# A fused forward and backward kernel: the joint stage laid out with d on partitions, with `grad_out` transposed by DMA

## The chip, the cores and the metric

The kernel runs on one core of one Trainium2 chip. The metric is device time in microseconds (us), taken over several executions; the profiled span, from the first to the last instruction of one execution, is about 2 us shorter. Before the change three runs gave a median of 1255.49 us (1254.1 to 1255.69). Some executions of a kernel fall in a slower state; runs are called fast or slow accordingly, and only fast runs are compared here. A ratio is the mean time of one kernel's fast runs over the mean time of the other's fast runs of the same rounds, on the same chip. It is therefore not quite the ratio of the medians quoted beside it.

## The reference, cut to what matters

The kernel computes the output of a small transducer model and the gradients of all its inputs. Two strided convolutions with GELU turn `x` into `f` with 4000 rows of 256 per batch. Then comes the joint stage, and the backward pass of everything.

```python
B, T, D, K, U = 2, 16000, 256, 3, 8              # all tensors are bf16
def _fwd_reference(x, w1, w2, g, w_f, w_g, w_o):
    ...                                          # two convolutions with stride 2: f is [2, 4000, 256]
    fe = jnp.einsum("btd,de->bte", f, w_f)
    ge = jnp.einsum("bud,de->bue", g, w_g)
    j = jnp.tanh(fe[:, :, None, :] + ge[:, None, :, :])      # [2, 4000, 8, 256]
    return jnp.einsum("btud,dv->btuv", j, w_o)

def reference(x, w1, w2, g, w_f, w_g, w_o, grad_out):        # grad_out is [2, 4000, 8, 256]
    _out, _vjp = jax.vjp(_f, x, w1, w2, g, w_f, w_g, w_o)
    return (_out, *_vjp(grad_out))
```

For the joint stage this means five things per batch. The output is `j @ w_o`. The gradient of `j` is `grad_out @ w_o.T`. It is multiplied by `1 - j*j` (the kernel keeps the negative of this product and calls it NGZ). NGZ summed over `u` is the gradient of `fe`; NGZ summed over `t` is the gradient of `ge`. The gradient of `w_o` is `j.T @ grad_out`, summed over all rows.

## The kernel before

A chunk is 512 rows of `t` (`TBF`), a block is 128 rows; each batch has eight chunks. `JT` holds tanh with d on the 128 partitions and comes straight from ACT. Everything else was computed with t on partitions. So PE transposed both `JT` (to `JR`) and `grad_out` (`GO_R` to `GOT`), by matmuls with the identity into f32 PSUM tiles of 512 columns, which ACT and DVE copied out as bf16.

```python
    def pe_transpose4(ps_pool, dst_ap, srcs, eng=None):
        ps = ps_pool.tile([P, 4, P], FP32, name="tr4_ps")
        for j, src in enumerate(srcs):
            nc.tensor.matmul(ps[:, j, :], lhsT=src, rhs=ident[:], start=True, stop=True)     # L153
        ...
        if eng == "act":
            nc.scalar.copy(out=dst_ap, in_=ps[:])                                            # L158
        else:
            nc.vector.tensor_copy(out=dst_ap, in_=ps[:])                                     # L160
    ...
        ps_fe = ...tile_pool(name="ps_fe", bufs=1, ...)       # PSUM pools of the joint stage
        ps_oj = ...tile_pool(name="ps_oj", bufs=2, ...)       # shared by O_ps and GJ_ps
        ps_tr = ...tile_pool(name="ps_tr", bufs=2, ...)
        ...
        def emit_reductions(NGZ_tb, tbg):                     # sums over t, then over u
            for u in range(U):
                for dt in range(KT):
                    nc.tensor.matmul(NGGE_ps[:, dt, u:u + 1], lhsT=NGZ_tb[:, u, dt * P:(dt + 1) * P],
                                     rhs=ones[:, 0:1], start=..., stop=...)                  # L319
            for dt in range(KT):
                for u in range(U):
                    nc.tensor.matmul(NGFE_ps[:, dt, :], lhsT=NGZ_tb[:, u, dt * P:(dt + 1) * P],
                                     rhs=ident[:], start=(u == 0), stop=(u == U - 1))        # L325
            nc.scalar.copy(out=NGFE_T[:, :, tcol:tcol + P], in_=NGFE_ps[:])
        ...
            for tbl in range(ntb):                            # each block of 128 rows
                ...                                           # GO_R loaded by DMA
                for g_ in range(U // 2):
                    srcs = [JT[:, kt, tbl, 2 * g_ + j, :] for j in range(2) for kt in range(KT)]
                    pe_transpose4(ps_tr, JR[:, 2 * g_:2 * g_ + 2, :, :], srcs, eng=("act" if g_ % 2 == 0 else "dve"))
                nc.vector.tensor_tensor(out=JSQ[:], in0=JR[:], in1=JR[:], op=ALU.mult)
                for g_ in range(U // 2):
                    srcs = [GO_R[:, 2 * g_ + j, kt * P:(kt + 1) * P] for j in range(2) for kt in range(KT)]
                    pe_transpose4(ps_tr, GOT[:, 2 * g_:2 * g_ + 2, :, :], srcs, eng="dve")
                for up in range(U // 2):
                    O_ps = ps_oj.tile([P, 2, V], FP32, name="OJ_ps")
                    ...                  # 4 matmuls of 256 columns: JT x WO       L390
                    GJ_ps = ps_oj.tile([P, 2, D], FP32, name="OJ_ps")
                    ...                  # 4 matmuls of 256 columns: GOT x WOT     L396
                    ...                  # 4 matmuls of 256 columns: JR x GO_R, summed in GWO_ps   L402
                    nc.scalar.copy(out=OUT_SB[:, 2 * up:2 * up + 2, :], in_=O_ps[:])         # L405
                    nc.vector.scalar_tensor_tensor(out=NGZ[:, 2 * up:2 * up + 2, :],         # L406
                                                   in0=JSQ[...], scalar=1.0, in1=GJ_ps[:],
                                                   op0=ALU.subtract, op1=ALU.mult)
                    ...                  # reductions of the block before; tanh of the next chunk on ACT, L345
```

Of the kernel before, what the change touches and what calls it, by code (L numbers as in the profile page):

```python
# [21 lines left out]
def kernel(  # L22
# [19 lines left out]
    nc = tc.nc  # L42
# [95 lines left out]
    ACC_GWO = accp.tile([P, KT, V], FP32, name="ACC_GWO")  # L138
    NGGE_all = accp.tile([P, B, KT, U], FP32, name="NGGE_all")
    GR8 = accp.tile([U, B, D], BF16, name="GR8")  # L140
# [9 lines left out]
    def pe_transpose4(ps_pool, dst_ap, srcs, eng=None):  # L150
        ps = ps_pool.tile([P, 4, P], FP32, name="tr4_ps")
        for j, src in enumerate(srcs):
            nc.tensor.matmul(ps[:, j, :], lhsT=src, rhs=ident[:], start=True, stop=True)  # L153
        if eng is None:
            eng = "act" if tr_ctr[0] % 2 == 0 else "dve"
            tr_ctr[0] += 1
        if eng == "act":
            nc.scalar.copy(out=dst_ap, in_=ps[:])  # L158
        else:
            nc.vector.tensor_copy(out=dst_ap, in_=ps[:])  # L160

    def pe_transpose8(ps_pool, dst_ap, srcs, eng=None):
        ps = ps_pool.tile([P, 8, P], FP32, name="tr8_ps")
        for j, src in enumerate(srcs):
            nc.tensor.matmul(ps[:, j, :], lhsT=src, rhs=ident[:], start=True, stop=True)  # L165
        if eng is None:
            eng = "act" if tr_ctr[0] % 2 == 0 else "dve"
            tr_ctr[0] += 1
# [4 lines that stand above are left out]
# [20 lines left out]
    for b in range(B):  # L193
# [107 lines left out]
        jtp = cctx.enter_context(tc.tile_pool(name="jtp", bufs=2))  # L301
        jtb = cctx.enter_context(tc.tile_pool(name="jtb", bufs=3))
        jtb2 = cctx.enter_context(tc.tile_pool(name="jtb2", bufs=2))
        ps_fe = cctx.enter_context(tc.tile_pool(name="ps_fe", bufs=1, space=bass.MemoryType.PSUM))
        ps_oj = cctx.enter_context(tc.tile_pool(name="ps_oj", bufs=2, space=bass.MemoryType.PSUM))
        ps_tr = cctx.enter_context(tc.tile_pool(name="ps_tr", bufs=2, space=bass.MemoryType.PSUM))
        ps_red = cctx.enter_context(tc.tile_pool(name="ps_red", bufs=1, space=bass.MemoryType.PSUM))
        ps_gge = cctx.enter_context(tc.tile_pool(name="ps_gge", bufs=1, space=bass.MemoryType.PSUM))
        ps_gwo = cctx.enter_context(tc.tile_pool(name="ps_gwo", bufs=1, space=bass.MemoryType.PSUM))
        GWO_ps = ps_gwo.tile([P, KT, V], FP32, name="GWO_ps")  # L310
        NGGE_ps = ps_gge.tile([P, KT, U], FP32, name="NGGE_ps")
        acc_state = {"n": 0, "n_gge": 0}
        n_acc_total = n_tb_total * U * KT

        def emit_reductions(NGZ_tb, tbg):
            for u in range(U):
                for dt in range(KT):
                    n = acc_state["n_gge"]
                    nc.tensor.matmul(NGGE_ps[:, dt, u:u + 1], lhsT=NGZ_tb[:, u, dt * P:(dt + 1) * P],  # L319
                                     rhs=ones[:, 0:1], start=(n == 0), stop=(n == n_acc_total - 1))  # L320
                    acc_state["n_gge"] = n + 1
            NGFE_ps = ps_red.tile([P, KT, P], FP32, name="NGFE_ps")
            for dt in range(KT):
                for u in range(U):
                    nc.tensor.matmul(NGFE_ps[:, dt, :], lhsT=NGZ_tb[:, u, dt * P:(dt + 1) * P],  # L325
                                     rhs=ident[:], start=(u == 0), stop=(u == U - 1))
            tcol = tbg * P
            nc.scalar.copy(out=NGFE_T[:, :, tcol:tcol + P], in_=NGFE_ps[:])

        def emit_fe(jc):  # L330
            t0 = jc * TBF
            JT = jtp.tile([P, KT, NTB, U, P], BF16, name="JT")
            fes = []
            for mt in range(KT):
                FE_ps = ps_fe.tile([P, TBF], FP32, name="FE_ps")
                for kt in range(KT):
                    nc.tensor.matmul(FE_ps[:, :], lhsT=WF[:, kt, mt * P:(mt + 1) * P],
                                     rhs=FT[:, kt, t0:t0 + TBF], start=(kt == 0), stop=(kt == KT - 1))
                fes.append(FE_ps)
            return JT, fes  # L340

        def tanh_gen(JT, fes):
            for mt in range(KT):
                for u in range(U):
                    nc.scalar.activation(out=JT[:, mt, :, u, :],  # L345
                                         in_=fes[mt][:, :].rearrange("p (tb t) -> p tb t", t=P),
                                         func=ACT.Tanh, bias=GE[:, mt, u:u + 1], scale=1.0)
                    yield

        JT_cur, fes = emit_fe(0)  # L350
        for _ in tanh_gen(JT_cur, fes):
            pass
        pending = None
        for jc in range(n_jchunks):
            ntb = NTB
            JT = JT_cur
            if jc + 1 < n_jchunks:
                JT_next, fes_next = emit_fe(jc + 1)
                tgen = tanh_gen(JT_next, fes_next)
            else:  # L360
                JT_next, tgen = None, None
            n_tanh_per_tb = (KT * U + ntb - 1) // ntb
            for tbl in range(ntb):
                tbg = jc * NTB + tbl
                tg0 = tbg * P
                Mv = max(0, min(P, MQ - tg0))
                GO_R = jtb.tile([P, U, V], BF16, name="GO_R")
                if Mv < P:
                    nc.gpsimd.memset(GO_R[:], 0.0)
                if Mv > 0:  # L370
                    nc.gpsimd.dma_start(out=GO_R[:Mv].rearrange("p u v -> p (u v)"),  # L371
                                        in_=grad_out[b, tg0:tg0 + Mv].rearrange("t u v -> t (u v)"))
                JR = jtb.tile([P, U, KT, P], BF16, name="JR")
                for g_ in range(U // 2):
                    srcs = [JT[:, kt, tbl, 2 * g_ + j, :] for j in range(2) for kt in range(KT)]
                    pe_transpose4(ps_tr, JR[:, 2 * g_:2 * g_ + 2, :, :], srcs, eng=("act" if g_ % 2 == 0 else "dve"))
                JSQ = jtb2.tile([P, U, KT, P], BF16, name="JSQ")
                nc.vector.tensor_tensor(out=JSQ[:], in0=JR[:], in1=JR[:], op=ALU.mult)
                GOT = jtb.tile([P, U, KT, P], BF16, name="GOT")
                for g_ in range(U // 2):  # L380
                    srcs = [GO_R[:, 2 * g_ + j, kt * P:(kt + 1) * P] for j in range(2) for kt in range(KT)]
                    pe_transpose4(ps_tr, GOT[:, 2 * g_:2 * g_ + 2, :, :], srcs, eng="dve")
                OUT_SB = jtb.tile([P, U, V], BF16, name="OUT_SB")
                NGZ = jtb.tile([P, U, D], BF16, name="NGZ")
                for up in range(U // 2):
                    O_ps = ps_oj.tile([P, 2, V], FP32, name="OJ_ps")
                    for j in range(2):
                        u = 2 * up + j
                        for kt in range(KT):
                            nc.tensor.matmul(O_ps[:, j, :], lhsT=JT[:, kt, tbl, u, :], rhs=WO[:, kt, :],  # L390
                                             start=(kt == 0), stop=(kt == KT - 1))
                    GJ_ps = ps_oj.tile([P, 2, D], FP32, name="OJ_ps")
                    for j in range(2):
                        u = 2 * up + j
                        for kt in range(KT):
                            nc.tensor.matmul(GJ_ps[:, j, :], lhsT=GOT[:, u, kt, :], rhs=WOT[:, kt, :],  # L396
                                             start=(kt == 0), stop=(kt == KT - 1))
                    for j in range(2):
                        u = 2 * up + j
                        for dt in range(KT):  # L400
                            n = acc_state["n"]
                            nc.tensor.matmul(GWO_ps[:, dt, :], lhsT=JR[:, u, dt, :], rhs=GO_R[:, u, :],  # L402
                                             start=(n == 0), stop=(n == n_acc_total - 1))
                            acc_state["n"] = n + 1
# [18 lines left out]
            if tgen is not None:  # L423
                for _ in tgen:
                    pass
# [270 lines left out]
```

## Time and profile before

| Reading | Value |
|---|---|
| Median of the runs | 1255.49 us |
| Joint stages (138–447 and 744–1052 us) | 309 and 308 us, half the span |
| PE busy in the first of them | 297 of 309 us |
| DVE, ACT, DMA in it | 239 us, 190 us, 30% |
| Joint stage per 512 rows | 37.03 us |

The joint stage's pace is read from the starts of the `GWO_ps` matmuls of successive chunks in the steady part of the stage. All paces below are taken this way. Successive chunks of before alternate between 36.2 and 37.3 us, so its mean comes out anywhere between 36.6 and 37.1 us, depending on the block that one counts from; 37.03 lies at the upper end, and sums built on it are good to about 0.3 us.

The page's first two parts show the busy time of each engine over the whole span, and the span in 40 slices (tenths of busy time, and the granted clock of PE). Profile of before:

```profile
PE 1090.8 (87%) x11147; PEld 861.4 (69%) x11196; DVE 859.9 (69%) x1254; ACT 648.3 (52%) x1023; POOL 190.6 (15%) x346
...
PE   3865599999999988799987749999999998878995
...
DVE  2999488778888875333369977787878887734232
...
PEclk9998599999999999999999978999999999999998
DMA  9766233233242264146447323333333224622552
```

PE shows nines in the two joint stages (slices 6 to 14 and 25 to 33, counted from 1), the clock has its top digit there but for an 8 in slice 25, and DMA is at 2 to 4 tenths in the first of them. The view by stretches gives the same in numbers. Its columns are the stretch in us, its length, then busy time and instruction count of PE, PE's weight loads, DVE, ACT and POOL, then granted clock, DMA share and GB/s. Before, the two joint stages; the stage behind each is called D here:

```profile
138.00:447.00 309.00, 297.43 (x3607) 256.72 (x3623) 238.67 (x356) 189.80 (x353) 36.46 (x66) 0.97 0.30 108
744.00:1052.00 308.00, 295.74 (x3605) 256.24 (x3621) 242.15 (x360) 190.75 (x354) 37.31 (x68) 0.98 0.31 109
```

The groups of instructions give the durations that the prediction is built of: busy us, mean ns of one, and the idle time of the engine before them with what ended it. Before:

```profile
L405 ACT CAST OUT_SB<-OJ_ps 128x512 bf16<-128x512 f32 x256 | 152.4, 595 | 155.8 <-PE OJ_ps L390 149.1
L406 DVE SCALAR_TENSOR_TENSOR NGZ<-JSQ,OJ_ps 128x512 bf16<-128x512 bf16 x256 | 169.6, 682 | 83.2 <-PE OJ_ps L396 83.0
L345 ACT ACTIVATE JT<-FE_ps,GE 128x512 bf16<-128x512 f32 x256 | 163.7, 723 | 12.4 <-PE NGFE_ps L325 5.0
L160 DVE CAST GOT<-tr_ps 128x512 bf16<-128x512 f32 x256 | 165.5, 683 | 3.9 <-PE tr_ps L153 2.1
L402 PE MATMUL GWO_ps<-GO_R,JR 128*128 128x256 bf16 x1024 | 164.5, 275 | 0.3
L170 ACT CAST FNg<-tr_ps 128x1024 bf16<-128x1024 f32 x32 | 32.4, 1012 | 146.5 <-PE tr_ps L165 146.5
L172 DVE CAST GFR<-tr_ps 128x1024 bf16<-128x1024 f32 x32 | 39.2, 1224 | 68.9 <-PE tr_ps L165 68.9
```

DVE spends 165.5 us of the two stages on nothing but copying transposed `grad_out` out of PSUM. PE's mean of 275 ns is the length of one 256-column matmul's record, whose end is modelled; the starts are 109 ns apart, and the starts are what a sum of work must use.

### The profile page before, as it was taken

Reading aid. Unit: us, or ns where it says so; the run is one execution under the profiler, and the core shown is the slowest. Engines: PE = TensorE matmul, PEld = TensorE weight load, DVE = VectorE, ACT = ScalarE, POOL = GpSimd, SP = SyncE. Lnnn points to the kernel's source line nnn. Section 1 sums busy time; section 2 is a strip of 40 time slices with the busy share of each in tenths; the row PEclk is TensorE's granted clock in tenths of the full one; section 3 lists DMA queues with packets and bytes.
Section 4 is the critical chain, followed back from the end, with each engine's and each line's share of the span. In section 5 each row is a group of like instructions: output and inputs, shape, how many; then the busy total and the mean of one; then the engine's idle time right before and its main releaser. Section 6 shows DMA issues by size and latency. Waiting matters only on the chain.

```text
span 1253.1 us, 26205 instructions
## 1 busy us (share of the span) xinstructions
PE 1090.8 (87%) x11147; PEld 861.4 (69%) x11196; DVE 859.9 (69%) x1254; ACT 648.3 (52%) x1023; POOL 190.6 (15%) x346
## 2 busy tenths in 40 slices
PE   3865599999999988799987749999999998878995
PEld 1333388888888845688843327888888885567884
DVE  2999488778888875333369977787878887734232
ACT  2887656676555401222258877666556642022223
POOL 0122011111111101023211211111111110101331
PEclk9998599999999999999999978999999999999998
DMA  9766233233242264146447323333333224622552
GB/s 175 188 180 175 80 114 124 103 109 129 102 134 103 90 225 150 51 136 205 149 106 191 116 107 121 117 121 111 127 111 126 102 105 148 226 70 78 197 190 83
DMA packets 122517, 165.27 MB, mean 132 GB/s; under 512 B 74304, under 2 KB 91232, under 8 KB 122400
## 3 DMA queue, kind: packets, MB, share of 16 engines
q0 software_dynamic: 34304, 123.39, 28.1%
q1 hardware_dynamic: 88096, 40.20, 13.1%
q8 instruction: 87, 1.43, 0.5%
q14 instruction: 30, 0.25, 0.1%
HBM read 75.41 MB, written 71.31 MB: 117 GB/s over the span
## 4 chain that ended last, share of the span: by engine, by line
PE 67%; DVE 16%; ACT 9%; issue 6%; DMA 2%; SPq 1%; another core or an unknown queue 0%; DVEq 0%; POOL 0%; ACTq 0%; POOLq 0%
PE tr_ps L153 9%; PE OJ_ps L390 9%; PE OJ_ps L396 8%; PE GWO_ps L402 8%; PE psE_t L594 7%; PE NGFE_ps L325 5%; DVE g_inner L178 3%; PE tr_ps L165 3%; ACT JT L345 3%; ACT FNg L170 3%; PE psA_t L245 2%; DVE g_rr L189 2%; PE NGGE_ps L319 2%; DVE g_oms L190 2%; PE GWF_ps L546 2%
## 5 line engine op out<-in xcount | busy, mean ns | idle before, releaser
L405 ACT CAST OUT_SB<-OJ_ps 128x512 bf16<-128x512 f32 x256 | 152.4, 595 | 155.8 <-PE OJ_ps L390 149.1
L406 DVE SCALAR_TENSOR_TENSOR NGZ<-JSQ,OJ_ps 128x512 bf16<-128x512 bf16 x256 | 169.6, 682 | 83.2 <-PE OJ_ps L396 83.0
L345 ACT ACTIVATE JT<-FE_ps,GE 128x512 bf16<-128x512 f32 x256 | 163.7, 723 | 12.4 <-PE NGFE_ps L325 5.0
L160 DVE CAST GOT<-tr_ps 128x512 bf16<-128x512 f32 x256 | 165.5, 683 | 3.9 <-PE tr_ps L153 2.1
L402 PE MATMUL GWO_ps<-GO_R,JR 128*128 128x256 bf16 x1024 | 164.5, 275 | 0.3
L390 PE MATMUL OJ_ps<-WO,JT 128*128 128x256 bf16 x1024 | 160.6, 273 | 4.9 <-ACT JT L345 1.5
L396 PE MATMUL OJ_ps<-WOT,GOT 128*128 128x256 bf16 x1024 | 154.0, 272 | 0.7
L600 DVE CAST GX_SB<-psE_t 128x512 bf16<-128x512 f32 x64 | 44.2, 691 | 125.7 <-ACT GX_SB L598 76.0
L245 PE MATMUL psA_t<-XC,W_81 128*128 128x512 bf16 (+1 forms) x377 | 93.7, 400 | 37.2 <-DVE HTe L182 18.3
L160 DVE CAST JR<-tr_ps 128x512 bf16<-128x512 f32 x128 | 88.0, 687 | 42.4 <-PE tr_ps L153 40.7
L390 PEld LDWEIGHTS <-JT 128*128 128x128 bf16 x1024 | 96.3, 98 | 27.7 <-issue 10.5
L153 PE MATMUL tr_ps<-ident,JT 128*128 128x128 bf16 x1024 | 101.6, 221 | 10.1 <-ACT JT L345 4.3
L170 ACT CAST FNg<-tr_ps 128x1024 bf16<-128x1024 f32 x32 | 32.4, 1012 | 146.5 <-PE tr_ps L165 146.5
L598 ACT CAST GX_SB<-psE_t 128x512 bf16<-128x512 f32 x64 | 37.5, 587 | 130.2 <-PE psE_t L594 87.4
L396 PEld LDWEIGHTS <-GOT 128*128 128x128 bf16 x1024 | 93.7, 98 | 13.0 <-issue 0.6
L153 PE MATMUL tr_ps<-ident,GO_R 128*128 128x128 bf16 x1024 | 99.7, 220 | 0.6 <-ACT JR L158 0.2
L402 PEld LDWEIGHTS <-JR 128*128 128x128 bf16 x1024 | 93.7, 99 | 8.4
L153 PEld LDWEIGHTS <-JT 128*128 128x128 bf16 x1024 | 77.6, 98 | 29.1 <-ACT JT L345 13.2
L245 PEld LDWEIGHTS <-W_81 128*128 128x128 bf16 x384 | 38.9, 102 | 83.1 <-issue 40.6
L371 POOL DMA_DIRECT2D GO_R<-in_grad_out_dram x64 | 34.4, 539 | 399.6 <-PE GWO_ps L402 312.0
L172 DVE CAST GFR<-tr_ps 128x1024 bf16<-128x1024 f32 x32 | 39.2, 1224 | 68.9 <-PE tr_ps L165 68.9
L325 PE MATMUL NGFE_ps<-ident,NGZ 128*128 128x128 bf16 x1024 | 86.3, 219 | 0.0
(761 smaller groups left out, 2138.2 us busy)
## 6 DMA issues: line engine op xcount, KB each, us to landing
GO_R<-in_grad_out_dram POOLq DMA_DIRECT2D x62, 512.0 KB, 3.6
out_dram<-OUT_SB POOLq DMA_DIRECT2D x62, 512.0 KB, 3.5
out_dram<-GX_SB POOLq DMA_DIRECT2D x62, 256.0 KB, 2.4
G1D<-G1c_w POOLq DMA_DIRECT2D x32, 256.0 KB, 2.6
HRD<-HRc POOLq DMA_DIRECT2D x16, 512.0 KB, 3.1
G1c<-G1D SPq DMA_DIRECT2D x32, 256.0 KB, 4.8
HRg<-HRD SPq DMA_DIRECT2D x16, 512.0 KB, 3.5
G2D<-G2c_w POOLq DMA_DIRECT2D x16, 256.0 KB, 2.6
```

The lines of the kernel that those rows point to most:

```text
L153: nc.tensor.matmul(ps[:, j, :], lhsT=src, rhs=ident[:], start=True, stop=True)
L160: nc.vector.tensor_copy(out=dst_ap, in_=ps[:])
L170: nc.scalar.copy(out=dst_ap, in_=ps[:])
L245: nc.tensor.matmul(ps[:, mt, :W], lhsT=W1[:, i, kt, mt * P:(mt + 1) * P], rhs=XC[:, c, kt, j:j + W], start=(k == 0), stop=(k == nmm - 1))
L325: nc.tensor.matmul(NGFE_ps[:, dt, :], lhsT=NGZ_tb[:, u, dt * P:(dt + 1) * P], rhs=ident[:], start=(u == 0), stop=(u == U - 1))
L345: nc.scalar.activation(out=JT[:, mt, :, u, :], in_=fes[mt][:, :].rearrange("p (tb t) -> p tb t", t=P), func=ACT.Tanh, bias=GE[:, mt, u:u + ...
L390: nc.tensor.matmul(O_ps[:, j, :], lhsT=JT[:, kt, tbl, u, :], rhs=WO[:, kt, :], start=(kt == 0), stop=(kt == KT - 1))
L396: nc.tensor.matmul(GJ_ps[:, j, :], lhsT=GOT[:, u, kt, :], rhs=WOT[:, kt, :], start=(kt == 0), stop=(kt == KT - 1))
L402: nc.tensor.matmul(GWO_ps[:, dt, :], lhsT=JR[:, u, dt, :], rhs=GO_R[:, u, :], start=(n == 0), stop=(n == n_acc_total - 1))
L405: nc.scalar.copy(out=OUT_SB[:, 2 * up:2 * up + 2, :], in_=O_ps[:])
L406: nc.vector.scalar_tensor_tensor(out=NGZ[:, 2 * up:2 * up + 2, :], in0=JSQ[:, 2 * up:2 * up + 2].rearrange("p u k d -> p (u k d)"), scalar ...
L594: nc.tensor.matmul(ps[:Mq, cj, :], lhsT=SRC[:, kt, q0 + sh:q0 + sh + Mq], rhs=W1T[:, i, kt, :], start=(k == 0), stop=(k == nmm - 1))
```

## The change

The intent is to give PE and DVE less to do in the joint stage. NGZ is computed with d on partitions, where `JT` already lies. `grad_out` transposed comes from a second load by DMA transpose, so PE does not transpose it and DVE does not copy it. The output gradient is then a matmul of 512 columns with the weights stationary. The sum over t becomes the accumulator output (`accum_out`) of the NGZ instruction instead of one-column matmuls. The transposes that remain write bf16 into PSUM, eight to a tile. The diff, cut to its core:

```diff
-    def pe_transpose4(ps_pool, dst_ap, srcs, eng=None):
...
     def pe_transpose8(ps_pool, dst_ap, srcs, eng=None):
-        ps = ps_pool.tile([P, 8, P], FP32, name="tr8_ps")
+        ps = ps_pool.tile([P, 8, P], BF16, name="tr8_ps")
         for j, src in enumerate(srcs):
-            nc.tensor.matmul(ps[:, j, :], lhsT=src, rhs=ident[:], start=True, stop=True)
+            nc.tensor.transpose(out=ps[:, j, :], in_=src, identity=ident[:])
...
+        gotp = cctx.enter_context(tc.tile_pool(name="gotp", bufs=2))
+        ps_gj = ...bufs=2    # GJ and FE share it
+        ps_o = ...bufs=2
+        ps_tr = ...bufs=1
+        ps_sum = ...bufs=2
+        def load_got(jc):
+            GOT = gotp.tile([P, KT, U, TBF], BF16, name="GOT")
             for u in range(U):
+                nc.sync.dma_start_transpose(out=GOT[:, :, u, :W], in_=grad_out[b, t0:t0 + W, u, :])
...
+        def half_block(jc, JT, hb, st):      # 128 rows, 4 of the 8 u
+            tr = ps_tr.tile([P, UH, KT, P], BF16, name="jr_ps")
+            ...                              # 8 transposes of JT
+            nc.vector.tensor_copy(out=JR[:Mv], in_=tr[:Mv])
+            ...                              # the output, as before
+        def emit_gwo(JR, GO_R, hf, Mv):      # as before, but one half block later
...
+            def emit_sum(dt, u, NGZ):
+                nc.tensor.matmul(sum_ps[dt][:, :W], lhsT=ident[:], rhs=NGZ[:, :W],
+                                 start=(u == 0), stop=(u == U - 1))
+            for step in range(KT * U):
+                for kt in range(KT):
+                    nc.tensor.matmul(gj_ps[:, :W], lhsT=WOT[:, kt, dt * P:(dt + 1) * P],
+                                     rhs=GOT[:, kt, u, :W], start=(kt == 0), stop=(kt == KT - 1))
+                nc.vector.tensor_tensor(out=JSQ[:, :W], in0=JT[:, dt, u, :W], in1=JT[:, dt, u, :W], op=ALU.mult)
+                nc.vector.scalar_tensor_tensor(out=NGZ[:, :W], in0=JSQ[:, :W], scalar=1.0, in1=gj_ps[:, :W],
+                                               op0=ALU.subtract, op1=ALU.mult,
+                                               accum_out=NGGE_parts[:, b, dt, u, jc:jc + 1])
+                sum_pend.append((dt, u, NGZ))
+                if len(sum_pend) > 2:
+                    emit_sum(*sum_pend.pop(0))
+                if step % 2 == 0:
+                    nxt = half_block(jc, JT, step // 2, st)
+                else:
+                    if gwo_pend is not None:
+                        emit_gwo(*gwo_pend)
+                    gwo_pend = nxt
+                next(tgen, None)             # one tanh of the next chunk
```

The last chunk now handles 416 rows where before padded it to 512. And the products of one step are used a step or two later in program order.

## The prediction

> **What bounds it now.** By the table of stretches the joint stage takes about 308 us in each of the two batches (138 to 447 and 745 to 1052 us), 616 of 1253. In it PE is busy 296 of 305 us, DVE 238, ACT 187, DMA 30%. The chain of waits between 150 and 230 us is over 80% PE (transposes 19%, the two output products 34%, GWO 16%, the sums 12%). So the joint stage is bound by PE, with DVE second. It moves at about 9.4 us per block of 128 rows, 37.5 per 512 rows.
>
> **PE.** Start-to-start times from the timeline: 128 columns 0.056 us, 256 columns 0.109, a one-column sum 0.025; 512 columns 0.216 by their difference. Per 512 rows, before: O, GJ, GWO 64 each (20.9 us), 192 transposes and NGFE sums (10.7), 64 one-column sums (1.6), FE 0.9: 34 us; the other 3.4 us are stalls. After: O and GWO 14.0, GJ as 32 of 512 columns 6.9, JT transposes 3.6, sums as 16 of 512 columns 3.5, FE 0.9: 28.8 us. Removed: grad_out transposes and one-column sums. Wider matmuls alone save little; they stream the same columns.
>
> **DVE.** Per 512 rows before: 16 GOT evictions of 0.683, 8 JR of 0.687, 16 NGZ of 0.682, 4 JSQ of 1.215: 32 us. After: no GOT; 16 JSQ of 128x512, about 0.42 each (estimate from 1.215 for 2048 elements and a fixed 0.15); 16 NGZ of 0.68 plus the accumulator read, which the Trainium skill ("VectorE: DVE Perf Modes", Two Vector instructions with no wait between them) counts as a second instruction, my estimate 0.1; 8 JR copies of 1024 elements; two NGFE copies of 0.68. An f32 eviction of 1024 takes 1.22 in this trace (GFR). The same page (the perf-mode tier table) lets a copy out of PSUM run at up to 2x, 1x for fp32; so with bf16 in PSUM I estimate 0.69. This trace has no large bf16 eviction to show it. Sum about 26 us, under PE's 28.8; at 1.22 it would be 30 and DVE would bind.
>
> **ACT** 16 tanh of 0.72 and 16 copies of 0.60: 21 us, not binding. **DMA:** 2.1 MB more per 512 rows by transposes. The x transposes used 256-byte packets at 22 ns each, so 11 us of 16 engines, beside 11.5 for grad_out and output: about 75% busy, not binding, landings slower. The loads are issued a chunk ahead.
>
> **Stalls.** FE shares two PSUM buffers with GJ and holds one until its eight tanh are done; in that time GJ has one buffer, and one GJ per FE waits on ACT, by hand about 0.7 us. I expect 30 to 31 us per 512 rows, plus about 10 us at the stage's start for the first tanh: about 256 us per batch against 308. Elsewhere bf16 transposes shorten DVE's GFR copies, but ACT's FNg copy (1.01 us) ends most waits there: 0 to 3 us per batch. Conv and E stay.
>
> **Predicted:** 1255 - 2x51 - 2 = 1151 us, range 1120 to 1185. Faster by over 2% 0.97, within 0.025, slower 0.005.
>
> **What would show it.** Joint stages of 250 to 262 us; PE still above 90% busy there; JR copies 0.69; NGZ 0.75 to 0.85; JSQ 0.42; DMA 65 to 80% in the stage; matmul count down by about 3,300; D and E stretches within 3 us.
>
> **What would make it wrong.** JR copies at 1.2 us, or a dear accumulator read: DVE-bound, 32 to 34 us per 512 rows, total 1180 to 1200. DMA transposes slowed by the plain traffic: PE waiting on GOT or GO_R. A lower granted PE clock, if transposes count less as activity. No stalls at all: 1120.

## More of the kernel before

PE "busy 297 of 309" hides one more thing. The records of matmuls overlap, because their ends are modelled, so small pauses between starts do not appear as idle time. Here is one in the timeline of before (start, length, engine, line, operation, count; idle before and its releaser in brackets). First PE:

```profile
196.15 0.61 PE L153 MATMUL tr_ps<-ident,JT 128*128 128x128 bf16 x8
196.94 0.60 PE L390 MATMUL OJ_ps<-WO,JT 128*128 128x256 bf16 x4 [0.18 <-ACT OUT_SB L405]
```

and ACT in the same microsecond:

```profile
195.15 1.27 ACT L345 ACTIVATE JT<-FE_ps,GE 128x512 bf16<-128x512 f32 x2 [0.42 <-PE NGFE_ps L325]
196.30 0.59 ACT L405 CAST OUT_SB<-OJ_ps 128x512 bf16<-128x512 f32 x1
```

Eight transposes at 56 ns should have been followed at 196.60. The next matmuls write an `OJ_ps` buffer and started at 196.94, 50 ns after ACT had copied one out (196.30 + 0.59), and ACT had first to finish two tanh.

## The result, and the profile after

| | Before, same rounds | After |
|---|---|---|
| Median of 4 runs, all fast | 1255.59 us | 1123.36 us |
| Range | 1254.1–1258.77 | 1115.07–1128.51 |
| Ratio of the fast runs (95%) | | 0.8935 (0.8888–0.8983) |
| Profiled span | 1253.1 us | 1113.3 us |
| Joint stage per 512 rows | 37.03 us | 28.83 us |

The change is a clear gain, 132 us by the medians. The after kernel spreads more than before: 13 us between its runs against 5. The profile is of the fastest of them.

The page of after, first two parts:

```profile
PE 966.8 (87%) x7790; PEld 689.8 (62%) x7868; DVE 728.1 (65%) x1476; ACT 550.6 (49%) x831; POOL 188.0 (17%) x346
...
PE   3876589999999987799987765999999999779995
...
DVE  2999768888888761323279994788888879223322
...
PEclk9999689999999999999999986999999999999997
DMA  8767499889894572066357428988898737414552
```

The matmul count fell by 3,357, as foreseen (about 3,300). DMA, which was at 2 to 4 tenths in the first joint stage, is now mostly at 8 to 9. By stretches, after, the two joint stages and the steady part of the first:

```profile
139.00:374.00 235.00, 229.42 (x1905) 167.97 (x1932) 183.74 (x462) 140.19 (x256) 33.95 (x63) 0.98 0.87 209
669.00:915.00 246.00, 231.78 (x1906) 169.31 (x1935) 188.01 (x469) 142.32 (x258) 35.81 (x66) 0.96 0.80 203
160.00:365.00 205.00, 203.63 (x1721) 151.71 (x1747) 166.54 (x419) 119.34 (x219) 30.71 (x57) 1.00 0.87 214
```

By these round windows the stages take 235 and 246 us where before took 309 and 308. The windows do not end where the stages do: D's first matmul starts at 445.3 and 1050.4 us in before, and at 376.5 and 917.0 in after. Read to there, the stages take 307.3 and 306.4 us before and 237.5 and 248.0 after. That is 128 of the 140 us between the two profiled spans. D, from its first matmul to the first of the stage behind it, took 93.8 and 93.6 us before and 89.3 and 88.8 after, 9.3 us less in the two batches. Most of that is the wait of DVE for D's first `G2c` load in each batch, in the view of the tile G2c (us, times), before, then after:

```profile
  DVE GF_T L462: 9.2, 2
```

```profile
  DVE GF_T L453: 2.8, 2
```

In the steady part of the joint stage (the last line of the stretches) PE is busy 203.6 of 205 us, DVE 166.5.

Groups of after that answer to those of before:

```profile
L407 DVE SCALAR_TENSOR_TENSOR NGZ<-JSQ,gj_ps 128x512 bf16<-128x512 bf16 (+1 forms) x256 | 172.5, 674 | 87.6 <-PE gj_ps L402 68.8
L162 ACT COPY FNg<-tr_ps 128x1024 bf16<-128x1024 bf16 x32 | 32.4, 1012 | 142.5 <-PE tr_ps L157 142.5
L405 DVE TENSOR_TENSOR JSQ<-JT 128x512 bf16<-128x512 bf16 (+1 forms) x256 | 105.6, 414 | 14.8 <-ACT JT L321 2.4
L345 DVE COPY JR<-jr_ps 128x1024 bf16<-128x1024 bf16 (+1 forms) x128 | 88.3, 690 | 2.5 <-DMA GO_R<-in_grad_out_dram 1.9
L164 DVE COPY GFR<-tr_ps 128x1024 bf16<-128x1024 bf16 x32 | 22.1, 692 | 84.0 <-PE tr_ps L157 84.0
```

With bf16 in PSUM, DVE copies 1024 elements per partition in 690 ns; from f32 it took 1224. This agrees with the Trainium skill ("VectorE: DVE Perf Modes", the perf-mode tier table), which allows a copy out of PSUM up to twice the rate and none of it for fp32. ACT gained nothing: FNg took 1012 ns from either type.

The view of one tile, NGZ of after, gives the price of `accum_out` (count, then minimum, median and maximum in ns):

```profile
L407 DVE SCALAR_TENSOR_TENSOR NGZ<-JSQ,gj_ps x256: 576/687/690, 145.8 to 914.5; 128x512 bf16<-128x512 bf16 x112, 128x416 bf16<-128x416 bf16 x16
L407 DVE DVE_READ_ACCUMULATOR NGZ<-JSQ,gj_ps x256: 81/83/84, 146.4 to 915.0; 128x1 f32 x128
```

The second instruction that the Trainium skill speaks of (same page, Two Vector instructions with no wait between them) is there in the trace, and costs 83 ns.

The DMA view of after over 160 to 365 us gives packets, MB and the share of 16 engines for each queue; q1 carries the transposes, q0 the plain loads and stores:

```profile
q1 hardware_dynamic: 56512, 14.02, 43.8%
q0 software_dynamic: 8121, 29.53, 43.0%
```

Per MB the transposes take 43.8/14.02 = 3.1% of the engines in this stretch, the plain transfers 43.0/29.53 = 1.5%. That is 2.1 times as much time for a transposed byte. It does not show that transposing is slow, because the transposes move in packets of 256 bytes and the plain loads in packets of 4096. In the packet records of after, from 138 to 445 us, the median is 18 ns for a transposed packet of 256 bytes, and 46 and 159 ns for plain packets of 1024 and 4096. A straight line through the two plain ones gives an estimate of 17.8 ns for a plain packet of 256 bytes. The means (26.2 and 51.0 ns, and 195 to 199 by queue) are less clear: the same line through them gives an estimate of 14 ns. The Trainium skill says the transposes are as fast as regular DMAs ("Advanced Engine Details and Errata", X-Bar Transpose). Per byte they are not; for their packet size they are by the medians and not by the means. No run had plain packets of 256 bytes, so this stays open.

### The profile page after: what moved, and what is told of

It is laid out like the page before. It is cut to its first block, busy times and chain, and to the rows that moved or that the text cites. A ratio compares the mean times of both kernels' runs of the same rounds, so it can differ in the third digit from the quotient of the medians.

```text
span 1113.3 us, 19863 instructions
## 1 busy us (share of the span) xinstructions
PE 966.8 (87%) x7790; PEld 689.8 (62%) x7868; DVE 728.1 (65%) x1476; ACT 550.6 (49%) x831; POOL 188.0 (17%) x346
## 4 chain that ended last, share of the span: by engine, by line
PE 65%; DVE 12%; ACT 4%; issue 3%; DMA 3%; SPq 1%; ACTq 0%; POOL 0%; DVEq 0%; POOLq 0%
PE O_ps L351 10%; PE GWO_ps L367 10%; PE gj_ps L402 9%; PE psE_t L585 8%; PE sum_ps L393 5%; PE jr_ps L342 5%; ACT FNg L162 3%; PE tr_ps L157 3%; PE GWF_ps L537 2%; DVE g_inner L170 2%; DVE g_rr L181 1%; DVE GH_To L476 1%; DVE GF_T L453 1%; DVE GH_Te L467 1%; DVE g_oms L182 1%
## 5 line engine op out<-in xcount | busy, mean ns | idle before, releaser
L354 ACT CAST OUT_SB<-O_ps 128x512 bf16<-128x512 f32 (+1 forms) x256 | 139.3, 602 | 196.3 <-PE O_ps L351 96.5
L407 DVE SCALAR_TENSOR_TENSOR NGZ<-JSQ,gj_ps 128x512 bf16<-128x512 bf16 (+1 forms) x256 | 172.5, 674 | 87.6 <-PE gj_ps L402 68.8
L321 ACT ACTIVATE JT<-gj_ps,GE 128x512 bf16<-128x512 f32 (+1 forms) x256 | 155.2, 719 | 2.4 <-remote 1.5
L402 PE MATMUL gj_ps<-GOT,WOT 128*128 128x512 bf16 (+1 forms) x469 | 142.5, 378 | 8.8 <-DMA GOT<-in_grad_out_dram 5.9
L351 PE MATMUL O_ps<-WO,JT 128*128 128x256 bf16 (+1 forms) x1024 | 137.7, 276 | 3.1 <-ACT JT L321 3.1
L367 PE MATMUL GWO_ps<-GO_R,JR 128*128 128x256 bf16 (+1 forms) x1024 | 134.4, 274 | 0.3 <-issue 0.2
L367 PEld LDWEIGHTS <-JR 128*128 128x128 bf16 (+1 forms) x1024 | 100.0, 98 | 38.8 <-issue 1.9
L405 DVE TENSOR_TENSOR JSQ<-JT 128x512 bf16<-128x512 bf16 (+1 forms) x256 | 105.6, 414 | 14.8 <-ACT JT L321 2.4
L351 PEld LDWEIGHTS <-JT 128*128 128x128 bf16 (+1 forms) x1024 | 95.9, 99 | 15.1 <-ACT JT L321 4.0
L162 ACT COPY FNg<-tr_ps 128x1024 bf16<-128x1024 bf16 x32 | 32.4, 1012 | 142.5 <-PE tr_ps L157 142.5
L393 PE MATMUL sum_ps<-NGZ,ident 128*128 128x512 bf16 (+1 forms) x254 | 93.1, 377 | 2.2
L342 PEld LDWEIGHTS <-JT 128*128 128x128 bf16 (+1 forms) x1024 | 68.9, 99 | 38.4 <-ACT JT L321 8.1
```

What stands on the lines that cost most here:

```text
L321: nc.scalar.activation(out=JT[:, mt, u, :W], in_=FE_ps[:, :W], func=ACT.Tanh, bias=GE[:, mt, u:u + 1], scale=1.0)
L342: nc.tensor.transpose(out=tr[:Mv, j, kt, :], in_=JT[:, kt, hf * UH + j, tb * P:tb * P + Mv], identity=ident[:])
L351: nc.tensor.matmul(O_ps[:Mv, jj, :], lhsT=JT[:, kt, u, tb * P:tb * P + Mv], rhs=WO[:, kt, :], start=(kt == 0), stop=(kt == KT - 1))
L354: nc.scalar.copy(out=OUT_SB[:Mv, u0:u0 + 2, :], in_=O_ps[:Mv])
L367: nc.tensor.matmul(GWO_ps[:, dt, :], lhsT=JR[:Mv, j, dt, :], rhs=GO_R[:Mv, hf * UH + j, :], start=(n == 0), stop=(n == n_gwo_total - 1))
L393: nc.tensor.matmul(sum_ps[dt][:, :W], lhsT=ident[:], rhs=NGZ[:, :W], start=(u == 0), stop=(u == U - 1))
```

## The experiments

Each kernel below was checked against the reference; a wrong result is said so. "Gaps" are a count from the trace: the time by which a matmul starts later than the usual spacing behind the one in front of it, summed over a steady stretch.

### Is it repeatable?

The same kernel as after, measured again (`a_again`).

> The changed kernel once more. The four timed runs were 1115, 1118, 1128 and 1128 us, a wider spread than the kernel before has (1254 to 1259). Theory: the spread sits in the first 15 to 25 us of the joint stage, where the first transposed grad_out loads meet other transfers (in the second batch PE stood 3.8 us for such a load); then the profile differs from the first one only between the end of the convolutions and about 25 us later, and the times lie between 1113 and 1130. Rival: the spread is in the granted clock over the whole run; then all stages are longer by the same share.

Measured: 1115.16, 1116.52 and 1114.69 us, and one slow run of 1134.39. Ratio 0.8883 (0.8868–0.8898). The gain stands, and the low end of the first measurement is the usual one. The profile was of an undisturbed run, so it cannot tell what a disturbed one loses.

### Does the bf16 copy out of PSUM matter in the joint stage?

The prediction said that DVE would bind if the JR copy took 1.2 us. This kernel makes it so: `a_f32tr`, after with JR transposed into f32 tiles again.

```diff
-            tr = ps_tr.tile([P, UH, KT, P], BF16, name="jr_ps")
-            ...nc.tensor.transpose(out=tr[:Mv, j, kt, :], ...)
-            nc.vector.tensor_copy(out=JR[:Mv], in_=tr[:Mv])
+            for jh in range(2):                  # two f32 tiles of 4 transposes; ps_tr bufs 2, ps_sum bufs 1
+                tr = ps_tr.tile([P, UH // 2, KT, P], FP32, name="jr_ps")
+                ...nc.tensor.matmul(tr[...], lhsT=JT[...], rhs=ident[:], start=True, stop=True)
+                nc.vector.tensor_copy(out=JR[:Mv, jh * (UH // 2):(jh + 1) * (UH // 2)], in_=tr[:Mv])
```

> The transposes of JT go to float32 in PSUM again, as two tiles of 512 elements per half block (one bank is taken from the sums for it). DVE then has two evictions of about 0.69 us in place of one, 5.5 us more per 512 rows, and comes to 28 us of 28. My prediction's theory: DVE binds then, 29.5 to 31 us per 512 rows, 25 to 45 us more in all (1145 to 1165). Rival: DVE has ample slack and the bf16 transposes gave nothing in this stage: within 8 us of the changed kernel.

Measured: 1116.37 us (1114.39–1117.91), ratio 0.8889 against 0.8883 for `a_again`: no difference. The stretch of its joint stage:

```profile
150.00:372.00 222.00, 219.82 (x1854) 163.15 (x1882) 207.27 (x512) 129.60 (x238) 32.20 (x60) 1.00 0.90 211
```

DVE is busy 207 of 222 us, 93%, and the pace is still 28.82 us per 512 rows. So DVE came close to PE and did not pass it. The fall-back in the prediction ("DVE-bound, 32 to 34 us") is refuted: DVE's work with f32 copies is 207.27/222 x 28.82 = 26.9 us per 512 rows, not 30.

### Does the accumulator output cost anything?

`a_noacc` drops `accum_out`. The sums over t are then zero, so two outputs are wrong.

```diff
                 nc.vector.scalar_tensor_tensor(out=NGZ[:, :W], in0=JSQ[:, :W], scalar=1.0, in1=gj_ps[:, :W],
-                                               op0=ALU.subtract, op1=ALU.mult,
-                                               accum_out=NGGE_parts[:, b, dt, u, jc:jc + 1])
+                                               op0=ALU.subtract, op1=ALU.mult)
```

> The accumulator output is left off (the sums over t are then zero, so grad g and grad w_g are wrong on purpose). DVE loses 128 accumulator reads of 0.083 us per batch, about 1.4 us per 512 rows. PE-bound theory: no change, within 6 us. Rival: the coupling of DVE and PE through two PSUM buffers limits, and any DVE time shows: 15 to 25 us faster.

Measured: 1118.93 us (1116.63–1132.94), ratio 0.8934 (0.8878–0.899): no gain. NGZ's own mean stayed at 674 ns. The 83 ns reads lie on an engine with slack. In this kernel the sum over t is free.

### Are the 512-column matmuls what gains?

`a_narrow` splits GJ and the u sums of after into matmuls of 128 columns.

```diff
-                    nc.tensor.matmul(gj_ps[:, :W], lhsT=WOT[...], rhs=GOT[:, kt, u, :W], ...)
+                for c in range(0, W, P):     # the u sums likewise
+                    nc.tensor.matmul(gj_ps[:, c:ce], lhsT=WOT[...], rhs=GOT[:, kt, u, c:ce], ...)
```

> The product with w_o transposed and the sums over u are cut into matmuls of 128 columns in place of 512: 192 matmuls per 512 rows in place of 48. By the start-to-start times of before (0.056 us for 128, 0.216 for 512) PE gains only 0.4 us per 512 rows: 0 to 10 us more in all. Rival: the wide matmuls are where the gain came from, because each matmul pays for a weight load of 0.098 us: 48 x 3 x 0.045, about 6.5 us per 512 rows, 80 to 110 us more.

Measured: 1126.76 us median (1124.47–1134.74), ratio 0.8985 (0.8949–0.902), about 12 us more than the fast runs of `a_again`. The pace is 29.2 us, 0.4 more per 512 rows, which makes 6 us in 16 chunks; the rest is no more than the spread of this layout's runs, and is not explained. The Trainium skill ("TensorE: Matmul & The Clock Gate", Wait — 56ns, not 53.3ns?) gives a fixed 2.5 ns for each matmul behind another. The spacings in this trace, 56 and 216 ns for 128 and 512 columns, agree: four narrow ones take 4 x 56 - 216 = 8 ns more. There are 48 such replacements per 512 rows, so 48 x 8 ns = 0.4 us, which is the pace's difference. Wide matmuls are a small term, as the prediction said.

The profiled run was the longest (1134.74) and shows one thing more. In the middle of its second joint stage everything stood still; the stretch of 5 us shows no instruction on any engine:

```profile
786.00:815.00 29.00, 27.27 (x362) 25.32 (x362) 22.83 (x57) 17.24 (x32) 4.30 (x8) 1.00 1.16 139
815.00:820.00 5.00, 0.00 (x0) 0.00 (x0) 0.00 (x0) 0.00 (x0) 0.00 (x0) 0.73 1.17 89
```

The profile names no releaser for PE's pause of 8.75 us around it, and the DMA share was no higher than in the 29 us in front. This chunk took 39.7 instead of 29.2 us, about what the run lost against the other three (6 to 10 us). It is one example of what a long run of the new layout loses. Why the engines stood still is open; that they waited for instructions behind crowded DMA queues is a guess that no run tests.

### What are before's gaps made of?

In before, 160 to 400 us, 145 gaps add up to 20.3 of 240 us. Twelve of them, 2.6 us, are no pauses: each is as long as one 512-column matmul (0.216 us), and 12 of the 24 FE matmuls of this stretch are missing from the trace. That leaves 133 gaps and 17.7 us, or 2.7 us of each 37.03. In after the same count gives 0.45 us in six places, and otherwise only such holes. The traces of the before variants below have all their FE matmuls. Three runs on before ask what the gaps depend on.

`b_nosum`: before with the one-column sums almost left out (two outputs wrong).

```diff
-                    nc.tensor.matmul(NGGE_ps[:, dt, u:u + 1], ...)
+                    if n < U * KT:
+                        nc.tensor.matmul(NGGE_ps[:, dt, u:u + 1], ...)
```

> The kernel before without its one-column sums over t (all but the first block's are dropped, so grad g and grad w_g are wrong on purpose): 1008 matmuls per batch of 0.024 us start to start are gone from PE, nothing from DVE. Theory that PE bounds the joint stage of before: its 24 us per batch come off, 40 to 50 us in all (1205 to 1215). Rival, that DVE's evictions and not PE's work set the pace of before: under 12 us.

Measured: 1241.81 us (1241.48–1244.59), ratio 0.9901 (0.9882–0.9921), 13 us less. Pace 36.23 us. Of the 1.6 us of PE work taken away per 512 rows, only 0.8 came back as time, and the gaps grew from 17.7 to 23.6 us, that is by 0.8 us per 512 rows. Neither forecast was met. The first one counted twice: the trace of before has 1024 of these sums in both batches together, and 32 of them stay, so PE's work alone would have given 992 x 0.025 = 25 us. About half of that was measured. Before's pace is thus PE's work plus waits, and the waits took back the other half.

`b_gotact`: before with half of the GOT copies on ACT, to take load off DVE.

```diff
-                    pe_transpose4(ps_tr, GOT[:, 2 * g_:2 * g_ + 2, :, :], srcs, eng="dve")
+                    pe_transpose4(ps_tr, GOT[...], srcs, eng=("act" if g_ % 2 == 0 else "dve"))
```

> The kernel before with every second eviction of transposed grad_out given to ACT: PE's work is the same, DVE loses 1.37 us per block of 128 rows (of about 7.5 busy of 9.2), ACT gains 1.2 (of 5.9). Between 160 and 400 us PE's matmul starts of before have about 20 us more than their usual spacing: 8%. If those gaps are DVE's doing (PE waits for evictions): 20 to 45 us less in all, the gaps in that stretch under 10 us. If PE's work alone sets the pace, or the gaps come from the order of work: within 8 us.

Measured: 1259.02 us (1257.67–1259.52), ratio 1.0022 (1.0004–1.004): no gain. Its stretch of 160 to 400 us, and the same of before, in two fences:

```profile
160.00:400.00 240.00, 237.15 (x2926) 204.42 (x2923) 167.74 (x234) 182.75 (x341) 27.37 (x51) 1.00 0.34 115
```

```profile
160.00:400.00 240.00, 237.40 (x2937) 207.56 (x2948) 193.66 (x288) 153.69 (x288) 28.45 (x53) 1.00 0.32 115
```

DVE went from 194 to 168 us, and the gaps did not shrink: 19.9 us against 17.7. So the gaps are not a matter of DVE's load.

`b_bf16`: before with bf16 transposes of eight to a tile, for JR and GOT.

```diff
-                for g_ in range(U // 2):         # 4 f32 transposes to a tile
-                    pe_transpose4(ps_tr, ...)
+                for g_ in range(U // 4):         # 8 bf16 transposes to a tile
+                    pe_transpose8b(ps_tr, ...)
```

> The kernel before with another part alone: in the joint stage the transposes of JT and grad_out go to bf16 in PSUM, eight to a bank, so 4 evictions per block of 128 rows in place of 8 (DVE 0.69 us each, ACT about 1.0). PE's work is the same. PE runs 37.0 us per 512 rows against 34 us of work. If the gaps come from the ring of two transpose tiles that PE has to wait for: 34.5 to 36 us per 512 rows, 16 to 40 us less in all (1215 to 1240). If they come from elsewhere in the order of work: within 8 us, as with the evictions given to ACT.

Measured: 1250.42 us (1249.64–1251.12), ratio 0.9956 (0.9935–0.9977), 5.5 us less; gaps 16.8 us, pace 36.68. Its stretch:

```profile
160.00:400.00 240.00, 236.49 (x2969) 208.26 (x2967) 154.21 (x211) 152.51 (x262) 28.45 (x53) 1.00 0.34 115
```

DVE fell from 194 to 154 us of 240, level with ACT, and little came of it.

With these traces in hand the gaps can be matched with the evictions. In before, all 133 gaps end 40 to 60 ns after the end of a copy or other read of PSUM by ACT or DVE, like the one shown above. By chance about one in twenty should, as some 580 DVE and ACT instructions end in 240 us. Summed by what ended just before, before's 17.7 us are: 8.3 us OUT_SB copies and 5.8 us JR copies, both on ACT; 1.7 us DVE's copies; 1.4 us tanh; 0.6 us NGZ. So the gaps are waits for a free PSUM buffer, mostly for an ACT copy. ACT is only 64% busy there (153.7 of 240), so it is not throughput. In part it is order: of the 14.0 us behind OUT_SB and JR copies, 5.1 follow a copy that began right behind a tanh in ACT's queue, and 3.7 one right behind another copy. The other 5.2 us follow a copy that ACT began from idle, so there the copy itself, with only two buffers in turn, made PE wait. In `b_gotact` the same count shows the waits moved rather than removed: 11.4 us for ACT's copies of transposes, 4.9 us for OUT_SB, both on ACT again. In `b_bf16` they moved to NGZ (7.8 us) and DVE's copies (3.6 us). In `b_nosum` DVE's copies rose to 6.5 us. The Trainium skill describes such a picture ("Perfetto Trace Analysis", Optimization Strategy): the same gap over and over on the engine that should be saturated can mean that there is no room in PSUM for the next tile. The trace of before agrees. Which of the new layout's properties ends these waits (separate pools for O, GJ and sums, wider tiles, or work put off by a step) was not tried one by one.

### What does grad_out by DMA gain alone?

`b_dmat`: before, and only its GOT by DMA transpose; all else with t on partitions. (To fit SBUF, OUT_SB has two buffers and JSQ one.)

```diff
-                    srcs = [GO_R[:, 2 * g_ + j, kt * P:(kt + 1) * P] for j in range(2) for kt in range(KT)]
-                    pe_transpose4(ps_tr, GOT[:, 2 * g_:2 * g_ + 2, :, :], srcs, eng="dve")
+            for u in range(U):               # once per chunk, one chunk ahead
+                nc.sync.dma_start_transpose(out=GOT[:, :, u, :W], in_=grad_out[b, t0:t0 + W, u, :])
```

> The kernel before with one part of the change alone: grad_out transposed by DMA, the product and the sums in the old layout (OUT_SB has two buffers and JSQ one, to fit). PE loses 1024 transposes (3.6 us per 512 rows), DVE 256 evictions of 0.68 us (10.9 per 512 rows). If this part frees both PE's work and its gaps: 3.6 + 3 us per 512 rows, 90 to 110 us less (1145 to 1165), most of the change's gain. If only PE's work counts: 50 to 60 us less (1195 to 1205).

Measured: 1193.04 us (1190.95–1195.62), ratio 0.9499 (0.948–0.9519), 63.5 us less. The pace fell from 37.03 to 32.35 us. Its stretch:

```profile
160.00:400.00 240.00, 237.36 (x2883) 207.55 (x2881) 156.55 (x209) 169.21 (x314) 34.23 (x60) 1.00 0.82 184
```

Per 512 rows, 64 transposes of 56 ns are 3.6 us, and the gaps fell from 2.7 to 13.4/240 x 32.35 = 1.8 us; together 4.5, against a measured 4.7. The buffers that had to be cut are not told apart from the load in this. The account closes on PE alone; it needs nothing from the 37 us that DVE has less to do in the stretch than before. What counts is PE's work and what PE waits for.

### Three changes to after

`a_pool` moves part of the u sums to POOL: it adds pairs of NGZ, so PE needs half the sum matmuls.

```diff
+                    nc.gpsimd.tensor_tensor(out=NGZ2[:, :W], in0=NGZ_even[:, :W], in1=NGZ[:, :W], op=ALU.add)
+                    sum_pend.append((dt, u - 1, NGZ2))      # one sum matmul for two u
```

> Pairs of NGZ tiles are added by the idle POOL in bf16 before PE sums them, so PE does 8 sums of 512 columns per 512 rows in place of 16. If PE alone bounds the joint stage: 1.7 us per 512 rows less, 25 to 30 us in all (1088 to 1095). Rival: POOL's adds of 128x512 take over 3.4 us or slow DVE down, then PE waits for them: no gain or a loss.

Measured: 1131.2 us (fast runs 1129.55–1132.74, one slow 1147.93), ratio 0.9002 (0.8979–0.9026): 15 us worse than `a_again`, though PE has less to do. Its joint stage, and JSQ in the view of one tile:

```profile
170.00:370.00 200.00, 187.41 (x1603) 137.97 (x1601) 194.99 (x392) 111.90 (x206) 89.94 (x108) 1.00 0.85 205
...
L406 DVE TENSOR_TENSOR JSQ<-JT x256: 357/426/1762, 141.5 to 926.6; 128x512 bf16<-128x512 bf16 x112, 128x416 bf16<-128x416 bf16 x16
```

JSQ takes up to 1762 ns. Its mean in the groups is 840 ns, where after has 414. DVE is now the busiest engine, 195 of 200 us, and the pace is 29.89. The Trainium skill states ("SBUF — State Buffer", Who interferes with whom) that a DVE instruction with two SBUF inputs contends with a POOL instruction that reads SBUF. JSQ reads two, the add reads two, and this trace agrees: of the full-size JSQ, the 118 that no add overlaps take 407 to 427 ns, and the 106 that overlap one have a median of 1406. An add takes 1128 ns on average. NGZ, which reads only one tile from SBUF, kept its time (663 ns on average against 674), but hardly ever ran beside an add. The move that PE's profile invites is refused by DVE.

`a_early` asks about the start of the second joint stage. After waits there once for GOT; timeline of PE, after:

```profile
692.30 1.03 PE L402 MATMUL gj_ps<-GOT,WOT 128*128 128x512 bf16 x2 [3.80 <-DMA GOT<-in_grad_out_dram]
```

The edit gives the first GOT and JT tiles buffers of their own in another order, so that they lie over memory which the stage in front frees sooner.

```diff
-        jtp = cctx.enter_context(tc.tile_pool(name="jtp", bufs=2))
-        gotp = cctx.enter_context(tc.tile_pool(name="gotp", bufs=2))
+        gotp = [cctx.enter_context(tc.tile_pool(name="gotp0", bufs=1))]
+        jtp = [cctx.enter_context(tc.tile_pool(name=f"jtp{i}", bufs=1)) for i in range(2)]
+        gotp.append(cctx.enter_context(tc.tile_pool(name="gotp1", bufs=1)))
```

> Same work; the first GOT and JT tiles are put where the convolution's outputs HTe and HTo lay, not where its gelu scratch lay, so the first transposed loads may go about 7 us earlier. If the stage's start is held by those loads: 8 to 20 us less in all, the first GOT load of the second batch issued about 668 and not 675 us, no PE wait on GOT in the profile, and the timed runs lie closer together than 1115 to 1134. If the start is held by the sixteen tanh of ACT: under 4 us.

Measured: 1109.77 us (1109.55–1109.91), ratio 0.8844 (0.8829–0.8859), 5 to 6 us less than `a_again` (by the ratios and by the medians). The first GOT of the second batch is issued at 668.63 us instead of 674.93, the wait of 3.80 us is gone, and the first chunk there takes 29.9 instead of 36.2 us. So the loads did hold that start, but the gain lies between the two forecasts. Its four runs lie within 0.4 us.

`a_d3b3` uses PSUM that the bf16 transposes freed in stage D: the transposes there get a third buffer.

```diff
-                tc.tile_pool(name="psD3t", bufs=2, space=bass.MemoryType.PSUM) as psD3t:
+                tc.tile_pool(name="psD3t", bufs=3, space=bass.MemoryType.PSUM) as psD3t:
```

> A third PSUM buffer for the transposes in the stage that forms grad w2 and grad w_f; the bank is there only because bf16 transposes take one bank in place of two. PE waits 22 us for ACT's FNg copies there, and a third buffer lets it transpose ahead: 4 to 14 us less in all, the stage about 50 us per batch in place of 54 to 56. Rival: the copies themselves are the pace: no change, within 3 us.

Measured: 1097.48 us (1095.51–1099.21), ratio 0.8746 (0.8726–0.8765), 17 to 18 us less than `a_again` and more than the 4 to 14 expected. In the view of the tile FNg, the list of who waited for it (us, times), after first, then `a_d3b3`:

```profile
  PE GWF_ps L537: 22.0, 32
```

```profile
  PE GWF_ps L537: 4.1, 16
```

PE's wait for FNg is 18 us shorter. So the bf16 transposes, which gave almost nothing as faster copies, gave room for a buffer, and the buffer is what pays.

`a_both` has both edits.

> The changed kernel with the earlier first loads (alone 6 us less, and no spread) and the third PSUM buffer (alone 18 us less). If the two are independent, as they lie in different stages: 1089 to 1095, spread under 3 us. If the earlier loads only shift a wait: 1096 to 1100.

Measured: the four fast runs 1089.34 to 1092.67 us, two slow ones of 1106.63 and 1118.73; ratio 0.8685 (0.8665–0.8705). The two gains add: 24 us below `a_again`'s fast median of 1115.2. This version beats both kernels. The forecast of a spread under 3 us was not met: slow runs remain, and their cause is open.

## Why the prediction was right or wrong

**Faster, and by how much: right.** Predicted 1151 us with a range of 1120 to 1185; measured 1123.36, within the range and near its low end. That it lies inside is partly luck: misses of opposite sign cancel in the sum (under "Joint stages" below).

**"The joint stage is bound by PE, with DVE second": right.** Taking 26 of 240 us off DVE in `b_gotact` gained nothing, taking 39 off in `b_bf16` gained 5.5 us over the whole kernel, and adding DVE work in `a_f32tr` cost nothing. For before it needs one addition: taking away PE work in `b_nosum` gave only half of it back, because PE also waited for PSUM buffers.

**"After ... 28.8 us" of PE work per 512 rows: right.** The pace is 28.83, and the granted clock stayed at 1.00 in the steady part.

**The stalls: the term that was mis-sized.** The prediction added to 28.8 an FE stall of "about 0.7 us" for each FE and expected "30 to 31 us per 512 rows". The runs show 28.83: no stall that counts. The difference, 1.2 to 2.2 us over 16 chunks, is 19 to 35 us, the largest of the misses. The FE matmuls of after, in PE's timeline, show why:

```profile
206.48 0.59 PE L318 MATMUL gj_ps<-FT,WF 128*128 128x512 bf16 x2
206.91 0.59 PE L402 MATMUL gj_ps<-GOT,WOT 128*128 128x512 bf16 x2
207.34 1.04 PE L367 MATMUL GWO_ps<-GO_R,JR 128*128 128x256 bf16 x8
208.29 0.59 PE L402 MATMUL gj_ps<-GOT,WOT 128*128 128x512 bf16 x2
```

FE takes one of the two buffers at 206.48, and GJ goes on with the other. Its next turn is due at 207.34 + 8 x 0.109 = 208.21 and comes at 208.29: it waits less than 0.1 us. ACT holds FE's buffer until 212.97 (its last two tanh start at 211.62 and last 1.35 us), but GJ needs only one buffer, because between two GJ there is almost a microsecond or more of other PE work in which NGZ (0.69 us) frees it. The hand model had GJ wait for ACT; in the trace it waits for NGZ, which is quick. The prediction did name this outcome under what would make it wrong ("No stalls at all: 1120").

**The same mistake on the other side: before's "3.4 us are stalls".** The size was a little high (2.7 by count), and the prediction added a stall of its own to the new kernel without asking what these were. They were waits for PSUM buffers, mostly for copies on ACT, and in the new layout they are gone. Per 512 rows the account closes: 37.03 less 3.6 for the grad_out transposes, 1.6 for the one-column sums, 0.2 for wider matmuls (by their spacings) and 2.7 for gaps is 28.9, against 28.83 measured.

**The DVE sum: "about 26 us", measured lower.** 166.54/205 x 28.83 = 23.4 us. The single durations were right: JR 0.69 (measured 0.690), JSQ 0.42 (0.416), NGZ with its read 0.75 to 0.85 (0.674 + 0.083 = 0.76). The records overlap from one instruction to the next (in these 205 us they add up to 184.5, with 166.5 busy), so their sum is too large. That is also why the f32 form came to 26.9 us and not 30. **ACT** was over-counted the same way: a tanh record is 0.72 us, but the 16 at the start of the stage took 9.37 us together, that is (9.37 - 0.72)/15 = 0.58 us from start to start.

**DMA "65 to 80%": wrong, it is 87% and 80%.** The estimate took 22 ns for a packet of 256 bytes, from the `x` transposes of before. Among the plain traffic the same packets took 25.9 ns, and the plain ones of 4096 bytes rose from 180.5 to 194.7. DMA still did not bind: PE's steady pace is its own.

**D "0 to 3 us per batch": a little low,** it was 4.6 and 4.7 us. The part it was about came out right: GFR fell to 692 ns, ACT's FNg of 1012 ns went on ending the waits, and the part of D with these copies takes 56.4 and 56.7 us before and 56.5 and 56.2 after. What it left out is the first `G2c` load, for which D waited 3 us less in each batch.

**Joint stages of 250 to 262 us: too long,** 237.5 and 248.0. The forecast of 256 fits eight full chunks of 30.75 us and 10 for the start. Measured are 4000/512 = 7.8 chunks of 28.83, 225 us, and 12 and 23 us for the start. So the stall term was 30 us too long in the two batches, and the short last chunk, which before padded, takes off another 12. The starts give 15 back, most of it in the second batch, with its 3.80 us wait for GOT and a first chunk of 36.2 us.

## What to carry to other kernels

Sum the bounding engine's work from start-to-start times and then find what its gaps wait for, matching their ends with the ends of evictions: here 2.7 us in 37 were waits for PSUM buffers, mostly behind an engine that was only 64% busy, and shifting load between DVE and ACT only moved them. Check first that a gap is not a record missing from the trace. Taking a transpose off PE by a second DMA load was worth its PE time here, although DMA's share of the first joint stage rose from 0.30 to 0.87. Memory that a change frees (a PSUM buffer in another stage) can be worth as much as the faster instruction that it was made for, so look for its use.

## What the Trainium skill lacked or had wrong

- "VectorE: DVE Perf Modes", Two Vector instructions with no wait between them, counts the accumulator read as an instruction but gives no time. It took 81 to 84 ns in all 256 cases.
- No page that was read gives the time from the end of an eviction to the start of the matmul that waited for its buffer. In before it was 40 to 60 ns, in 133 gaps.
- "SBUF — State Buffer", Who interferes with whom, gives the rule for two-input DVE instructions beside POOL, but no size for it. Here 128x512 bf16 squares took 407 to 427 ns alone, and 1406 (median) where they overlapped an add on POOL; 840 on average, 1762 at most.
